# Two pairs of projection blocks by seven products in tiles 3 to 6, and query copies on VectorE behind four strided transposing transfers, in a sparse-attention and bilinear-FFN kernel

## The chip, the cores and the metric

The kernel runs on one core of one Trainium2 chip. A core has TensorE (PE, matrix products into PSUM), VectorE (DVE), ScalarE (ACT) and GpSimd (POOL), and queues from which transfers are issued (here those of SyncE, SP, and of POOL). The metric is device time in microseconds (us), the median of several executions. The kernel before took 326.81 us (three runs: 325.43 to 327.33). One further execution was profiled.

## The reference

```python
# q, k, v: (8, 8, 576, 64); w_a, w_b: (512, 1536); w_out: (1536, 512)
scores = q @ k.T / 8
rel = pos[:, None] - pos[None, :]
mask_local   = (rel >= 0) & (rel < 32)                               # heads 0 to 3
mask_strided = (rel >= 0) & (pos[None, :] % 32 == pos[:, None] % 32) # heads 4 to 7
attn = softmax(where(mask, scores, -1e9))
x = (attn @ v), heads side by side, as (4608, 512)
out = ((x @ w_a) * (x @ w_b)) @ w_out
```

Products are taken in bf16 and summed in fp32.

## The kernel before

**Staging.** The 4608 tokens are nine FFN tiles of 512 (`NT`, t = 0 to 8). Attention runs by batch element b (576 tokens each). The transposed attention output goes into a ring `xT` of four batch elements, [128, 4, 2304], so tile 4 wraps round and its products are cut into 256 columns. The attention of batch b is spread, in small steps, over the FFN of tile b-1.

**The order is written by hand.** Inside the schedule block the program order is the order on each engine. A tile is 16 slots: 12 slots of `ffn_ab` (one 128-wide block f of d_ff each: eight products of 512 columns into two banks, a ScalarE copy `a_sb` of the one, L633, a VectorE product with the other into `pf`, L636) and 4 slots of the second projection (the "y" slots). After each slot, `take(i)` (L1057) emits the attention steps due there (`STEPS` for batches 1 and 2, `LATER` and `IN_Y` for the others, L570 to L578), and `at` holds loads and sums due at that slot (L1001 to L1044). From slot 14 on, POOL first copies one element of the slot's result into `pace` (L1054), so what POOL issues next waits for that slot.

**Attention steps.** S(u): scores into the two-bank tile `st` (L377), exp on ScalarE (L397), mask on VectorE (L415). V(u), u < 4: P times V into `o` (L454), reciprocal and scaling on VectorE (L462, L480). V(u), u >= 4 from batch 2 on is `step_VT`: the product transposed, into two banks `o` (L513), Ln and Exp of the sums on ScalarE (L523, L524), a VectorE product into `xT` (L527). O and I send the local heads' rows out to DRAM and back transposed (L495, L500). Q0 to Q3 are `step_Q`: from batch 2 on, queries arrive transposed by DMA (`step_D`, L320 and L323) in `qT` and POOL copies them into `qz`, whose other 64 partitions are zero: Q0 and Q1 the local heads (L335), Q2 and Q3 the strided heads in two pieces with a permutation of tokens (L333).

**Seven products.** The second projection in tiles 1 to 8 (`FAST_Y`) and the first projection's `w_a` half for some pairs of blocks in tiles 7 and 8 (`FAST_A`, `a_pair`, L667) use a 2 by 2 scheme with seven half-size products in place of eight. It needs sums of weights (`wsum_make`, L648, in tile 6), sums of x (`xsum_make`, L659), and, per pair, five ScalarE copies of 128x256 (L705 to L724), and adds (L713, L722 on VectorE, L717 on POOL). `fast_s` (L740) makes the sums of `pf` (`ps`) for the second projection.

**PSUM.** Eight banks: `st` two, `mm` three, `tp` one, `o` two. Projection banks come from `mm_bank` in turn: three `mm`, then `tp`.

Of the kernel before, what the change touches and what calls it, by code (L numbers as in the profile page):

```python
# [7 lines left out]
F32 = mybir.dt.float32  # L8
# [6 lines left out]
FIRST_D = 2  # L15
# [11 lines left out]
FAST_Y = (1, 2, 3, 4, 5, 6, 7, 8)  # L27
FAST_A = {7: (1, 2, 3, 4, 5), 8: (0, 1, 2, 3, 4, 5)}
# [3 lines left out]
def kernel(  # L32
# [44 lines left out]
    qz_pair = [(const.tile([128, 2, 2, S], BF16, name=f"qz{i}l"), const.tile([128, 2, RS, 2, NP], BF16, name=f"qz{i}s"))  # L77
               for i in range(2)]
    qz_buf = [[(l[:, :, j], s[:, :, :, j]) for j in range(2)] for l, s in qz_pair]
# [30 lines left out]
    def fill_v(t):  # L110
        nc.gpsimd.memset(t[:, :, :, D:] if len(t.shape) == 4 else t[:, :, D:], 1.0)
# [67 lines left out]

    def blocks(nm, z):  # L180
        z = int(z)
        return sb.tile([128, 2, (S, RS * GP)[z]], BF16, tag=f"t{nm}{z}", name=f"t{nm}{z}", bufs=1)
# [133 lines left out]
    def step_D(b, z, nm):  # L316

        rows = nats[b, nm, z == 1]
        if z == 0:
            nc.sync.dma_start(out=kT_buf[b % 2][0][:, :, PAD:] if nm == "k" else qT[0],  # L320
                              in_=rows.rearrange("t h d -> t (h d)"), transpose=True)
        else:
            nc.sync.dma_start(out=kT_strided(b)[:, :HL * W] if nm == "k" else qT[1],  # L323
                              in_=rows.rearrange("h (t e) d -> (h t) (e d)", e=2), transpose=True)

    def step_Q(b, z, j):

        r = slice(64 * j, 64 * j + 64)
        src = qT[z][r]
        if z:  # L330
            src = src.rearrange("d (c h p i) -> d c h i p", c=2, h=2, i=4)
            for c in range(2):
                nc.gpsimd.tensor_copy(qz_buf[b % 2][j][1][r, c].rearrange("d (h i) p -> d h i p", h=2), src[:, c])  # L333
        else:
            nc.gpsimd.tensor_copy(qz_buf[b % 2][j][0][r], src)  # L335
# [22 lines left out]
    def S_p(b, u):  # L358
        c, half, M, n, G = unit(u)
        kT = kT_buf[b % 2][c // 2]  # L360

        st = pst.tile([128, 2, 512], F32, tag="st", name="st")
        held[b, "st", u] = st
        if b > 0:
            sv = st.rearrange("p a (i n) -> p (a i) n", n=256)
            for i in range(G):
                k0 = (G * half + i) * (LW if c < 2 else GP)
                if c < 2:
                    rhs = qz_pair[b % 2][0][:, c % 2, :, k0:k0 + n]
                else:  # L370
                    rhs = qz_pair[b % 2][1][:, c % 2, G * half + i]
                if c < 2 or b < FIRST_D:
                    lhs = kT[:, c % 2, k0:k0 + 128]
                else:
                    k0 = W * (u - HL) + i
                    lhs = kT_strided(b)[:, k0:k0 + 509:4]
                nc.tensor.matmul(sv[:, i, :2 * n].rearrange("p (j n) -> p j n", j=2), lhsT=lhs, rhs=rhs, start=True, stop=True)  # L377
# [49 lines left out]
    def V_p(b, u):  # L427
        c, half, M, n, G = unit(u)
        p = ps.pop((b, u))
        if b == 0:  # L430

            o = psum4["o"].tile([128, 512], F32, tag="o", name="o")
            if c < 2:
                of = o[:, :2 * G * (D + 1)].rearrange("p (j g e) -> p j g e", j=2, e=D + 1)
                sm = of[:, :, :, D:]
            else:
                of = o.rearrange("p (j g e) -> p j g e", j=2, e=D)
                sm = psum4["sum"].tile([128, 2, 4, 1], F32, tag="sum", name="sum")
        else:
            o = psum4["o"].tile([128, 2, 512], F32, tag="o", name="o")  # L440
            of = o[:, :, :G * (D + 1)].rearrange("p j (g e) -> p j g e", e=D + 1)
            sm = of[:, :, :, D:]
# [59 lines left out]
    def step_VT(b, u):  # L502

        c, half, M, n, G = unit(u)
        p = ps.pop((b, u))
        o = psum4["o"].tile([128, 2, 512], F32, tag="o", name="o")
        for i in range(G):
            for j in range(2):
                if c < 2:
                    vt = vl_buf[b % 2][:, (2 * c + j) * 6 + 3 * half + i]  # L510
                else:
                    vt = vs_buf[b % 2][:, u - HL, 2 * i + j]
                nc.tensor.matmul(o[:, j, i * n:(i + 1) * n], lhsT=vt, rhs=p_cols(b, p, j, i, n, n)[:M], start=True, stop=True)  # L513

        r = sb.tile([128, RS * 4 * D], BF16, tag="xr", name="xr", bufs=2)[:64, :4 * W].bitcast(F32)
        r = r.rearrange("p (j w) -> p j w", j=2)
        if c < 2:
            sums = o[64:, :, :W]
        else:

            sums = o[64:, :, :W].rearrange("d j (i p) -> d p i j", p=NP)
            r = r.rearrange("d j w -> d (j w)").rearrange("d (p i j) -> d p i j", i=G, j=2)
        nc.scalar.activation(r, sums, ACT.Ln)  # L523
        nc.scalar.activation(r, r, ACT.Exp, scale=-1.0)  # L524
        if c >= 2:
            dst = xT[64 * (u % 2):64 * (u % 2) + 64, c, S * (b % XR):S * (b % XR + 1)]
            nc.vector.tensor_mul(dst.rearrange("d (p i j) -> d p i j", i=G, j=2),  # L527
                                 o[:64, :, :W].rearrange("d j (i p) -> d p i j", p=NP), r)
            return
        for j in range(2):  # L530
            dst = xT[64 * j:64 * j + 64, c, S * (b % XR):S * (b % XR + 1)]
            nc.vector.tensor_mul(dst[:, W * half:W * (half + 1)], o[:64, j, :W], r[:, j])
# [21 lines left out]
    def step_X(b, c):  # L554
# [20 lines left out]
    LATER = {-6: "Q0", -5: "Q1", -1: "S0", 0: "S1", 1: "V0 Q2", 2: "S2", 3: "V1 O0 Q3", 4: "S3 I0", 5: "V2", 6: "S4", 7: "V3 O1", 8: "S5", 9: "V4 I1",  # L575
# [39 lines left out]
    def ffn_ab(t, f, mid, ab=None):  # L615
# [3 lines left out]
        if f // 2 in FAST_A.get(t, ()):  # L619
            if f % 2 == 0:  # L620
                pairs[t, f // 2] = a_pair(t, f // 2)
            return next(pairs[t, f // 2])
# [9 lines left out]
        a_sb = fsb.tile([128, TTOK], F32, tag="a_sb", name="a_sb")  # L632
# [4 lines left out]
        else:  # L637
# [4 lines left out]
    wsum_a = [flat.rearrange("p (c g m) -> p c g m", c=2, g=FG)  # L642
              for flat in [vl_buf[0].rearrange("p a b -> p (a b)")[:, 12 * 128 * z:12 * 128 * (z + 1)] for z in range(2)]
              + [t[:, :12 * 128] for t in qz_flat[0]]]
    xsum = {t: qz_flat[1][t - 7][:, :8 * HT].rearrange("p (n c m) -> p n c m", n=4, c=2)
            for t in FAST_A}

    def wsum_make(n):  # L648
        w, s_ = (lambda e, j: wav[:, j, :, :, e]), wsum_a
        a, b, op = ((w(1, 0), w(1, 1), ALU.add), (s_[0], w(0, 0), ALU.subtract), (w(0, 0), w(1, 0), ALU.subtract),  # L650
                    (w(0, 1), s_[1], ALU.subtract))[n]
        for c in range(2):
            nc.vector.tensor_tensor(s_[n][:, c], a[:, c], b[:, c], op=op)

    def x_part(t, j, k):
        x0 = TTOK * t % (XR * S) + HT * k
        return xT[:, 2 * j:2 * j + 2, x0:x0 + HT]
# [8 lines left out]

    def a_pair(t, g):  # L667
# [3 lines left out]
        X = pool.tile([128, 2, 512], F32, tag=nm, name="ax")[:, 0, :HT]  # L671
        a = ([fsb.tile([128, TTOK], F32, tag="a_sb", name="a_sb") for _ in range(2)] if g % 2 == 0 else
# [155 lines left out]
    def y_tail(t):  # L828

        plan, y = products(t), y_bufs()  # L830
        banks = {("X", 1): psum4["o"].tile([128, 2, 512], F32, tag="o", name="end")[:, 0, :HN],
# [75 lines left out]
    with tc.manual_schedule(engines={ENG.PE, ENG.SP, ENG.Pool, ENG.DVE, ENG.Activation}):  # L907
# [72 lines left out]
        open_psum(ctx, mm=3, tp=1, o=1)  # L980
# [41 lines left out]
        for n in range(4):  # L1022
            do(16 * (NT - 3) + 2 * n + 2, wsum_make, n)
# [11 lines left out]
        do(28, fill_v, vs_buf[1])  # L1035
# [52 lines left out]
```

## Time and profile before

| what | value |
|---|---|
| median of three runs | 326.81 us |
| the profiled execution's own time | 326.64 us |
| its span, first to last instruction | 324.9 us |
| mean granted TensorE clock | 0.997 |
| PE busy | 315.5 us (97%) |
| VectorE busy | 234.1 us (72%) |
| ScalarE busy | 186.4 us (57%) |
| POOL busy | 150.1 us (46%) |
| chain that ended last: PE / VectorE / ScalarE | 89% / 4% / 2% |

A matmul's record includes its pipeline, so PE at 97% is not PE at its peak; durations of chains of matmuls are better read from the starts of successive pieces in the chain that ended last. Tile boundaries in that chain are at about 57.9 us (tile 1), 94.5 (tile 2), 128.4 (3), 161.8 (4), 195.9 (5), 229.6 (6) and 263.0 (7).

### The profile page before, as it was taken

Reading aid. Unit: us, or ns where it says so; the run is one execution under the profiler, and the core shown is the slowest. Engines: PE = TensorE matmul, PEld = TensorE weight load, DVE = VectorE, ACT = ScalarE, POOL = GpSimd, SP = SyncE. Lnnn points to the kernel's source line nnn. Section 1 sums busy time; section 2 is a strip of 40 time slices with the busy share of each in tenths; the row PEclk is TensorE's granted clock in tenths of the full one; section 3 lists DMA queues with packets and bytes.
Section 4 is the critical chain, followed back from the end, with each engine's and each line's share of the span. In section 5 each row is a group of like instructions: output and inputs, shape, how many; then the busy total and the mean of one; then the engine's idle time right before and its main releaser. Section 6 shows DMA issues by size and latency. Waiting matters only on the chain.

```text
span 324.9 us, 7111 instructions
## 1 busy us (share of the span) xinstructions
PE 315.5 (97%) x2706; PEld 214.2 (66%) x2734; DVE 234.1 (72%) x489; ACT 186.4 (57%) x331; POOL 150.1 (46%) x240
## 2 busy tenths in 40 slices
PE   8999999998999999999999999999999999999994
PEld 6754555454765578556999995559555866786684
DVE  6765786498956785688667766777699667857862
ACT  6763766454754476447644765467546655535541
POOL 8944922893785356524652565336124003202520
PEclk9999999999999999999999999999999999999998
DMA  8999999999699999999998999999863030004004
GB/s 150 155 204 196 204 187 204 204 126 175 87 132 153 191 129 101 131 207 167 102 104 181 158 107 107 158 182 112 59 101 103 2 113 17 3 2 129 0 3 129
DMA packets 127234, 40.40 MB, mean 124 GB/s; under 512 B 115040, under 2 KB 124320, under 8 KB 127008
## 3 DMA queue, kind: packets, MB, share of 16 engines
q0 software_dynamic: 80400, 19.28, 64.5%
q1 hardware_dynamic: 46656, 20.61, 36.3%
q8 instruction: 21, 0.34, 0.5%
q14 instruction: 13, 0.11, 0.1%
q10 hardware_dynamic: 144, 0.07, 0.1%
HBM read 39.12 MB, written 18.28 MB: 177 GB/s over the span
## 4 chain that ended last, share of the span: by engine, by line
PE 89%; DVE 4%; ACT 2%; issue 2%; DMA 2%; POOL 0%; ACTq 0%; POOLq 0%
PE mm L612 42%; PE mm L816 18%; PE mm L696 5%; PE st L377 4%; PE mm L878 3%; PE ax L689 3%; PE o L454 2%; PE mm L689 2%; PE o L513 2%; DMA shared<-in_q_dram 2%; PE mm L843 2%; PE end L843 1%; DVE p L415 1%; PE misc L156 1%; PE tp L540 1%
## 5 line engine op out<-in xcount | busy, mean ns | idle before, releaser
L612 PE MATMUL mm<-xT,wb_sb 128*128 128x512 bf16 (+1 forms) x381 | 88.0, 352 | 0.4
L612 PE MATMUL mm<-xT,wa_sb 128*128 128x512 bf16 (+1 forms) x367 | 86.6, 351 | 0.6
L633 ACT COPY a_sb<-mm 128x512 f32<-128x512 f32 x84 | 49.2, 585 | 47.1 <-PE mm L612 45.5
L636 DVE TENSOR_TENSOR pf<-a_sb,mm 128x512 bf16<-128x512 f32 x74 | 50.6, 684 | 26.0 <-PE mm L612 18.4
L612 PEld LDWEIGHTS <-wb_sb 128*128 128x128 bf16 x392 | 37.8, 98 | 33.7 <-issue 0.4
L1054 POOL CAST pace<-pf 1x1 f32<-1x1 bf16 x72 | 21.0, 291 | 77.0 <-DVE pf L636 47.8
L612 PEld LDWEIGHTS <-wa_sb 128*128 128x128 bf16 x392 | 34.9, 98 | 20.9
L397 ACT ACTIVATE p<-st 72x576 bf16<-72x576 f32 (+1 forms) x56 | 36.4, 650 | 20.1 <-PE st L377 19.8
L816 PEld LDWEIGHTS <-ps 128*128 128x128 bf16 x336 | 32.5, 98 | 4.6 <-issue 0.5
L527 DVE TENSOR_TENSOR xT<-o,xr 64x576 bf16<-64x576 f32 x24 | 18.0, 751 | 19.8 <-ACT xr L524 19.6
L816 PE MATMUL mm<-wf,ps 128*128 128x256 bf16 x252 | 30.1, 273 | 0.5 <-ACT y_sb L781 0.3
L781 ACT COPY y_sb<-mm 128x512 f32<-128x512 f32 (+1 forms) x32 | 17.9, 559 | 19.3 <-PE mm L816 16.6
L816 PEld LDWEIGHTS <-pf 128*128 128x128 bf16 x252 | 23.6, 98 | 2.7
L696 PE MATMUL mm<-xT,wb_sb 128*128 128x512 bf16 x83 | 25.3, 379 | 0.1
L816 PE MATMUL mm<-wo_sb,pf 128*128 128x256 bf16 x168 | 21.8, 273 | 0.0
L750 DVE TENSOR_TENSOR ps<-pf 128x512 bf16<-128x512 bf16 (+1 forms) x49 | 21.2, 433 | 0.7
L523 ACT ACTIVATE xr<-o 64x576 f32<-64x576 f32 x24 | 15.6, 648 | 9.4 <-PE o L513 9.2
L1054 POOL COPY pace<-y_sb 1x1 f32<-1x1 f32 x17 | 4.1, 241 | 36.0 <-ACT y_sb L887 13.3
L236 POOL DMA_DIRECT2D vs<-in_v_dram x24 | 20.4, 863 | 0.0
L415 DVE TENSOR_TENSOR p<-p,mask_s 72x576 int16<-72x576 int16 x28 | 18.7, 669 | 1.8 <-ACT p L397 1.5
L454 PEld LDWEIGHTS <-p 128*128 128x128 bf16 (+1 forms) x256 | 13.0, 97 | 8.9 <-DVE xl L480 2.1
L415 DVE TENSOR_TENSOR p<-p,mask_l 128x576 int16<-128x576 int16 x32 | 14.7, 458 | 4.3 <-ACT p L397 4.3
(183 smaller groups left out, 546.7 us busy)
## 6 DMA issues: line engine op xcount, KB each, us to landing
out_dram<-y_sb SPq DMA_DIRECT2D x14, 512.0 KB, 4.9
kr<-in_k_dram POOLq DMA_DIRECT2D x12, 288.0 KB, 5.8
qr<-in_q_dram POOLq DMA_DIRECT2D x12, 288.0 KB, 6.9
vl<-in_v_dram POOLq DMA_DIRECT2D x6, 384.0 KB, 9.5
out_dram<-y_sb SPq DMA_DIRECT2D x7, 256.0 KB, 4.1
vs<-in_v_dram POOLq DMA_DIRECT2D x24, 72.0 KB, 5.9
xd<-xl SPq DMA_DIRECT2D x12, 144.0 KB, 4.8
wo_sb<-in_moe_w_out_dram POOLq DMA_DIRECT2D x4, 384.0 KB, 10.4
```

Of the source, the lines that this page charges most:

```text
L236: nc.gpsimd.dma_start(out=vs_buf[b % 2][:, h, :, 0:D], in_=v[b, HL + h].rearrange("(p r) d -> p r d", r=RS))
L397: nc.scalar.activation(p_flat(p)[:M, :2 * W].rearrange("p (i n) -> p i n", n=2 * n), st[:M].rearrange("p a (i n) -> p (a i) n", n=256)[:, ...
L415: nc.vector.tensor_tensor(pi, pi, mk, op=ALU.bitwise_and)
L454: nc.tensor.matmul(of[:, j, i, :w], lhsT=pt, rhs=vt, start=True, stop=True)
L527: nc.vector.tensor_mul(dst.rearrange("d (p i j) -> d p i j", i=G, j=2), o[:64, :, :W].rearrange("d j (i p) -> d p i j", p=NP), r)
L612: nc.tensor.matmul(ps_[:, c0:c0 + n], lhsT=w[:, kk, 128 * f:128 * (f + 1)], rhs=xT[:, kk, x0:x0 + n], start=(kk == first and c0 == 0), sto ...
L633: nc.scalar.copy(a_sb, ab[0])
L636: nc.vector.tensor_mul(pf[:, f, :].rearrange("p (i a s) -> p a i s", i=2, s=16), halves(a_sb), halves(ab[1]))
L696: nc.tensor.matmul(got[e], lhsT=wb_sb[:, kk, 128 * f:128 * (f + 1)], rhs=xT[:, kk, x0:x0 + TTOK], start=kk == 0, stop=kk == KD - 1)
L750: nc.vector.tensor_tensor(s[:, n], a, b, op=op)
L816: nc.tensor.matmul(bank[b][:, q], lhsT=lhs(g, q), rhs=rhs(g), start=k in "172" and q == 0 and g == 0, stop=g == FG - 1, skip_group_check=True)
L1054: nc.gpsimd.tensor_copy(pace, done)
```

## The change

- `MID_A`: in tiles 3 to 6, block pairs g = 1 and 3 (f = 2, 3 and 6, 7) go through a new `a_pair_mid`, seven products for the `w_a` half. Its accumulating chain X is a 256-column tile in a bank of its own, tag `e`; all adds are on VectorE. Sums of x for these tiles are made in slot 16t-1 and 16t; sums of weights are made in tile 2 (slots 34 to 47) in place of tile 6, in buffers that attention used early.
- From slot 48 (tile 3) on, `o` is one bank, and `e` the other. `V_p` fits one bank then; `step_VT` writes its two halves to `o` and `e`, with two Ln and two products of half size. In all `step_VT` the loops of i and j change places.
- `step_Q` is one VectorE copy of 64x1152 for each of Q0 to Q3; the token permutation of the strided heads is now made by four transposing transfers of 288 rows each in place of one of 1152. `qz`'s strided part has another layout, and the scores read it accordingly.
- Q steps move: Q0, Q1 two slots later (into the y slots; batch 2: from 16.5 to 17), Q2, Q3 one slot later (batch 2: from 20 and 21 to 21.5 and 22). Three loads move by one slot; the memset of `vs`'s spare columns for the odd buffer moves from slot 28 to slot 2. `a_sb` has three buffers.

```diff
+MID_A = {t: (1, 3) for t in (3, 4, 5, 6)}
...
-    qz_pair = [(... name=f"qz{i}l"), const.tile([128, 2, RS, 2, NP], BF16, name=f"qz{i}s"))
+    qz_pair = [(... name=f"qz{i}l"), const.tile([128, 2, 2, RS, NP], BF16, name=f"qz{i}s"))
...
         else:
-            nc.sync.dma_start(out=kT_strided(b)[:, :HL * W] if nm == "k" else qT[1],
-                              in_=rows.rearrange("h (t e) d -> (h t) (e d)", e=2), transpose=True)
+            for i in range(4):
+                nc.sync.dma_start(out=qT[1][:, W * i:W * (i + 1)], transpose=True,
+                                  in_=rows.rearrange("h (p i e) d -> i (h p) (e d)", i=4, e=2)[i])
 
     def step_Q(b, z, j):
         r = slice(64 * j, 64 * j + 64)
-        src = qT[z][r]
-        if z:
-            src = src.rearrange("d (c h p i) -> d c h i p", c=2, h=2, i=4)
-            for c in range(2):
-                nc.gpsimd.tensor_copy(qz_buf[b % 2][j][1][r, c].rearrange("d (h i) p -> d h i p", h=2), src[:, c])
-        else:
-            nc.gpsimd.tensor_copy(qz_buf[b % 2][j][0][r], src)
+        dst = qz_buf[b % 2][j][z][r]
+        nc.vector.tensor_copy(dst.rearrange("d c r n -> d (c r n)") if z else dst, qT[z][r])
...
+        if "e" in psum4:
+            o = [psum4[nm].tile([128, 512], F32, tag=nm, name=nm) for nm in "oe"]
...
+        for j in range(2):
+            for i in range(G):
+                nc.tensor.matmul(o[j][:, i * n:(i + 1) * n], lhsT=vs_buf[b % 2][:, u - HL, 2 * i + j],
+                                 rhs=p_cols(b, p, j, i, n, n)[:M], start=True, stop=True)
...
+        for j in range(2):
+            nc.scalar.activation(by_token(r)[:, :, :, j], o[j][64:, :W].rearrange("d (i p) -> d p i", p=NP), ACT.Ln)
+        nc.scalar.activation(r, r, ACT.Exp, scale=-1.0)
+        for j in range(2):
+            nc.vector.tensor_mul(by_token(dst)[:, :, :, j], o[j][:64, :W].rearrange("d (i p) -> d p i", p=NP),
+                                 by_token(r)[:, :, :, j])
...
-             2: {16.5: "Q0 Q1", 20: "S0 Q2", 20.5: "S1", 21: "V0 Q3", 21.5: "S2", 22: "V1", 22.5: "S3 O0", ...
+             2: {17: "Q0 Q1", 20: "S0", 20.5: "S1", 21: "V0", 21.5: "S2 Q2", 22: "V1 Q3", 22.5: "S3 O0", ...
-    LATER = {-6: "Q0", -5: "Q1", -1: "S0", 0: "S1", 1: "V0 Q2", 2: "S2", 3: "V1 O0 Q3", 4: "S3 I0", ...
+    LATER = {-4: "Q0", -3: "Q1", -1: "S0", 0: "S1", 1: "V0", 2: "S2 Q2", 3: "V1 O0", 4: "S3 I0 Q3", ...
...
+    def a_pair_mid(t, g):
+        pf = pfs[t]
+        X = psum4["e"].tile([128, 512], F32, tag="e", name="e")[:, :HT]
+        Y, Z, b1, b0 = [mm_bank([128, TTOK]) for _ in range(4)]
...
+        P(Y, w(0, 1), x(1, 0), True)
+        P(X, w(0, 0), x(0, 0), True)
+        nc.scalar.copy(quarter(0, 0), X)
+        b_mm(b1, 1, (0, 1, 2))
+        P(X, ws(1), xs(1))
+        nc.scalar.copy(quarter(1, 0), X)
+        P(Z, ws(2), xs(2), True)
+        nc.scalar.copy(p7, Z)
+        b_mm(b1, 1, (3,))
+        add(quarter(0, 0), Y)
+        yield p7[:1, :1]
+        P(X, ws(0), xs(0))
+        nc.scalar.copy(quarter(1, 1), X)
+        b_mm(b0, 0, (0,))
+        P(Z, w(1, 1), xs(3))
+        add(quarter(1, 0), Z)
+        add(quarter(1, 1), p7)
+        b_mm(b0, 0, (1, 2, 3))
+        P(X, ws(3), x(1, 1))
+        nc.scalar.copy(quarter(0, 1), X)
+        mult(1, b1)
+        mult(0, b0)
+        yield pf[:1, 2 * g, :1]
...
-                do(15, load_vl, b)
+                do(14, load_vl, b)
-                do(17 if b == FIRST_D + 1 else g0 - 2, load_qk, b, False)
+                do(18 if b == FIRST_D + 1 else g0 - 2, load_qk, b, False)
...
         for n in range(4):
-            do(16 * (NT - 3) + 2 * n + 2, wsum_make, n)
+            for c in range(2):
+                do(16 * 2 + (2, 5, 7, 9, 11, 13, 14, 15)[2 * n + c], wsum_make, n, c)
+        for t in MID_A:
+            do(16 * t - 1, xsum_make, t, 0)
+            for n in (1, 2, 3):
+                do(16 * t, xsum_make, t, n)
...
-        do(28, fill_v, vs_buf[1])
+        do(2, fill_v, vs_buf[1])
...
+            elif i == 16 * min(MID_A):
+                outs.close()
+                open_psum(ctx, o=1, e=1)
```

Here P(bank, ...) is two products of 256 columns, `b_mm` one of 512 columns for each entry, `add` a VectorE sum of 128x256 fp32, `mult` the VectorE product into `pf`.

More of the change, by code (lines that the diff above doesn't have):

```diff
@@ L110, in fill_v @@
     def fill_v(t):
-        nc.gpsimd.memset(t[:, :, :, D:] if len(t.shape) == 4 else t[:, :, D:], 1.0)
+        nc.gpsimd.memset(t[:, :, :, D + 1:], 1.0)
     spare = const.tile([128, 2], BF16, name="spare")
@@ L505, in step_VT @@
         p = ps.pop((b, u))
[L506 to L513, printed above, removed]
-        r = sb.tile([128, RS * 4 * D], BF16, tag="xr", name="xr", bufs=2)[:64, :4 * W].bitcast(F32)
@@ L516, in step_VT @@
[L516 to L528, printed above, removed]
+        if "e" in psum4:
+            o = [psum4[nm].tile([128, 512], F32, tag=nm, name=nm) for nm in "oe"]
+        else:
+            o2 = psum4["o"].tile([128, 2, 512], F32, tag="o", name="o")
+            o = [o2[:, j] for j in range(2)]
@@ L631, in ffn_ab @@
                 ab_mm(t, f, ab, range(KD), mid)
-        a_sb = fsb.tile([128, TTOK], F32, tag="a_sb", name="a_sb")
+        a_sb = fsb.tile([128, TTOK], F32, tag="a_sb", name="a_sb", bufs=3)
         nc.scalar.copy(a_sb, ab[0])
@@ L670, in a_pair @@
         pool, nm = ((pst, "st"), (psum4["o"], "o"))[g % 2]
-        X = pool.tile([128, 2, 512], F32, tag=nm, name="ax")[:, 0, :HT]
-        a = ([fsb.tile([128, TTOK], F32, tag="a_sb", name="a_sb") for _ in range(2)] if g % 2 == 0 else
+        X = pool.tile([128, 512] if nm == "o" else [128, 2, 512], F32, tag=nm, name="ax")
+        X = X[:, :HT] if nm == "o" else X[:, 0, :HT]
+        a = ([fsb.tile([128, TTOK], F32, tag="a_sb", name="a_sb", bufs=3) for _ in range(2)] if g % 2 == 0 else
              [t.rearrange("p h n -> p (h n)")[:, :2 * TTOK].bitcast(F32) for t in kT_buf[0]])
@@ L830, in y_tail @@
         plan, y = products(t), y_bufs()
-        banks = {("X", 1): psum4["o"].tile([128, 2, 512], F32, tag="o", name="end")[:, 0, :HN],
+        banks = {("X", 1): psum4["o"].tile([128, 512], F32, tag="o", name="end")[:, :HN],
                  ("Z", 1): pst.tile([128, 2, 512], F32, tag="st", name="end")[:, 0, :HN]}
@@ L979 @@
         early.close()
-        open_psum(ctx, mm=3, tp=1, o=1)
+        open_psum(ctx, mm=3, tp=1)
+        outs = ExitStack()
+        open_psum(outs, o=1)
         slots = []
```

83 lines of the change are left out of this document (63 added, 20 removed), and 2 rows, old and new, of the table STEPS.

## The prediction

> **What bounds the kernel now.** I read the page's chain of waits first.
>
> ```profile
> PE 89%; DVE 4%; ACT 2%; issue 2%; DMA 2%; POOL 0%; ACTq 0%; POOLq 0%
> ```
>
> TensorE's own work sets the end, with two exceptions: the prologue, which the change leaves alone, and tile 1. So an edit can gain in two ways: fewer TensorE columns anywhere, or fewer TensorE waits in tile 1. The table of stages separates them (columns: stretch, its length, busy us and instructions of PE, PEld, DVE, ACT, POOL, granted clock, DMA share, GB/s):
>
> ```profile
> 68.00:74.50 6.50, 5.37 (x44) 2.89 (x44) 6.43 (x12) 3.34 (x6) 6.44 (x13) 1.00 1.90 126
> 82.90:94.50 11.60, 10.95 (x115) 9.32 (x112) 9.05 (x14) 7.27 (x13) 10.68 (x14) 1.00 1.31 119
> 94.50:117.90 23.40, 23.24 (x156) 12.17 (x158) 16.80 (x35) 13.05 (x22) 10.15 (x20) 1.00 1.38 154
> 117.90:128.40 10.50, 10.45 (x110) 9.32 (x108) 7.77 (x13) 7.37 (x12) 7.42 (x11) 1.00 1.37 100
> ```
>
> Rows 2 and 4 are the y slots of tiles 1 and 2, with the same TensorE work; tile 1 takes 11.6 us for them, tile 2 10.5. In row 1 TensorE idles 1.1 us while VectorE and POOL are both full. The timeline says why (start, us, engine, line, instruction; the bracket is idle time and its releaser):
>
> ```profile
> 70.42 2.04 DVE L750 TENSOR_TENSOR ps<-pf 128x512 bf16<-128x512 bf16 x1
> 70.67 1.50 POOL L333 COPY qz0s<-qTs 64x576 bf16<-64x576 bf16 x2
> 74.18 0.35 PE L454 MATMUL o<-vl,p 128*128 128x65 bf16 x6 [1.07 <-DVE xl L480]
> ...
> 83.17 1.52 DVE L415 TENSOR_TENSOR p<-p,mask_s 72x576 int16<-72x576 int16 x1
> 83.24 1.14 POOL L335 COPY qz1l<-qTl 64x1152 bf16<-64x1152 bf16 x1
> ...
> 100.00 1.35 POOL L333 COPY qz1s<-qTs 64x576 bf16<-64x576 bf16 x2 [3.35 <-DMA qTs<-qr]
> ```
>
> L750's median is 0.42 us and L415's with mask_s 0.45; beside a POOL query copy they take 2.04 and 1.52, as long as the copy runs and their own work after it. VectorE is then late and PE waits 1.07 us for it. The last row: POOL also waits for the transposed queries to land; today nobody waits for POOL there.
>
> **Part 1, the seven products.** A plain block is eight 512-column products, 1.73 us in the chain (row 137.88 below), so a pair is 3.46. Tile 7's seven-product pairs are the same mix of products; one piece of each pair recurs here:
>
> ```profile
> 137.88 1.73 PE mm L612 x8
> ...
> 266.48 0.65 PE mm L696 x3
> 269.74 0.65 PE mm L696 x3
> 272.99 0.65 PE mm L696 x3
> ```
>
> The distance is 3.26 us, so 0.20 less for each pair and 1.2 for six pairs; in tile 4, where all columns come in 256s (16 for 1.75 us, 0.109 each), 32 become 30, 0.22 less, for two pairs. Together 1.65 us off the path, if no copy is late. What is added beside it, for each pair: five ScalarE copies of 0.373 (L705 to L724) for two of 0.585, +0.70 us; VectorE adds 3 x 0.425 (L713, L722, L779 at 256 columns), +1.28. For each tile four sums of x, 4 x 0.42 (L663), +1.68. The weight sums, 8 x 0.55 (L653), move from tile 6 to tile 2. `step_VT` for batches 4 to 7: two Ln of 64x288 for one of 0.648: between 128x256 and 128x512 copies (0.373 and 0.585) the slope gives about 0.40 each, +0.15; two products for one of 0.751, about 0.43 each by the 256-column adds, +0.11. The third `a_sb` buffer, the bank split and the new loop order add no instruction on TensorE: zero, and there is nothing to uncover.
>
> The tightest place is the chain in the one-bank tile. In slot 3, X must be copied out before the last X product. ScalarE first does the exp of S2: it starts 0.44 us after the first score product (67.52 to 67.96), takes 0.65, then the copy 0.37, 1.5 us with a little signalling. TensorE in that time does the scores 0.30, two 256s 0.22, one 512 0.22, two 256s 0.22, three 512s 0.65, in all 1.6. Cover 0.1 us; the same in slot 7. Bounds: 0 (tile 7 shows none) to 0.65 for each of 8 (a whole exp in the way). I take 0.1 in all, since the cover is short but there. If the copy is late, the next is only the rest of this pair.
>
> **Part 2, the query copies.** POOL loses 32.5 us (L333 9.5 + 8.4, L335 7.3 + 7.3). VectorE gains 24 copies. No VectorE row has this shape; the nearest are L269's, 96x768 in bf16: 0.345 three times and 1.04 once. The once is beside POOL issuing transfers:
>
> ```profile
> 40.44 1.04 DVE L269 COPY tq<-shared 96x768 bf16<-96x768 bf16 x1
> ...
> 39.17 2.13 POOL L207 DMA_DIRECT2D qr<-in_q_dram  x1
> 40.27 1.55 POOL L205 DMA_DIRECT2D kr<-in_k_dram  x1
> ```
>
> So 0.35 to 1.14 (POOL's own time for 64x1152); I take 0.345 x 1152/768 = 0.52, since most rows are undisturbed. That is 2.1 us of VectorE for each batch, against about 1.0 to 1.6 of stretched masks and sums that go.
>
> The Trainium skill, "SBUF — State Buffer", section "Who interferes with whom", has this as an exclusive lock: a VectorE instruction with two SBUF inputs and a GpSimd one that reads SBUF shut each other out. Here the trace agrees (0.45 to 1.52). It goes on that VectorE's fast copies shut out descriptor generation too, whoever starts first, which speaks against the change; the 1.04 us row agrees. By it every Q copy that meets a load being issued would take about 1.0.
>
> In tile 1 VectorE is the limit twice. Around 70 to 74 it loses 1.62 (2.04 to 0.42) and 0.38 (L750 at 74.04 took 0.79) and gains two copies, 1.04: 0.96 less, so of the 1.07 us wait I take 0.95. In the y slots it loses 1.07 and 0.54 (L415 at 83.17 and 87.35) and gains Q0, Q1 of batch 3, 1.04: 0.57 less, so of the 1.1 us I take 0.6. Together 1.55; bounds 0 (the new copies fill the hole) and 2.2.
>
> From tile 2 on VectorE has 23.4 - 16.8 = 6.6 us free in slots 0 to 11. In tiles 3 to 6 it gets there 3 x 0.42 + 2 x 1.28 + 2 x 0.52 + 0.2 = 5.1; in tile 2, 5 x 0.55 + 1.04 = 3.8. That is cover, and the cost is nothing. Gone, it is `pf` and `ps` that come late, and the y products wait.
>
> **Part 3, the four transfers.** SP issues three more for each of six batches. Its rows: 1.30 to 1.67 us for 1152 rows, 1.15 for 576 (L500), so up to 3 x 1.15 = 3.5 us more of SP each time. Behind them on SP stands only the next tile's first store (from 92.8 to 103.6 in tile 1-2, later 128.1 to 137.2), so SP has room. But the copy Q2 needs all four, and now VectorE waits, with masks, `pf` and reciprocals queued behind. How much later the last lands is not shown. Below: nothing, as the bytes are the same. Above: 8.4 us, if each takes the 2.8 us that lay between the landings of kT0s and qTs (59.66 + 5.7 and 61.07 + 7.1). I take 1.5, by the 1.15 us issue of the nearest small one with landings overlapped. Slack of the old landing to the place where VectorE comes to Q2: batch 2, 68.2 to 71.3, 3.1; batch 3, 99.95 to about 101.5, less what tile 1 gains, about 1 (SP's chain moves up with it in part); batches 4, 6 and 7, about 3 (131.4, 199.2, 233.0 against slot ends of tile 3, 5, 6); batch 5 more. A VectorE halt of some 2 us costs nothing: the product of slot 3 (0.69) is needed by the second half of slot 5. So only batch 3 may pay: 0.2.
>
> **The moved loads and memset.** They sit on POOL, 46% busy before and less after; they land well ahead of use (kr of batch 3 is issued at 66.3, transposed at 71.6, read at 94.2). Zero; without that cover the transposes of the batch would slip one slot, about 2 us, against the same slack.
>
> **Sum.** 326.64 - 1.65 + 0.1 - 1.55 + 0.2 = 323.7; the profiled execution stands 0.17 under the median of 326.81, so I forecast 323.8.
>
> **Rivals.**
> - *Tile 1 loses all its waits:* 2.2 in place of 1.55, the chain tight but never late: 323.0 and, with the loads earlier on a freer POOL, down to 322.4. For: POOL is full there (6.44 of 6.50). Against: VectorE was full too and takes over the copies.
> - *Only one of the two gains arrives.* Either ScalarE's copies come late by 0.2 in each pair (the cover is 0.1), or VectorE's new copies are held by POOL's issuing (two more of 1.04) and fill tile 1's hole. Each gives 325.3 to 325.5. That the lockout merely changes its partner is how the change would not do what it says.
> - *VectorE stands before the query copies (slower).* If the last of four transfers lands 5.5 us later (nearly 2 us for each extra one), VectorE halts for 2.4 in batch 2, about 4.5 or more in batch 3 and 2.5 in 4, 6 and 7; less the 2.0 that banks allow, PE loses 0.4 + 2.5 to 3.5 + 3 x 0.5, about 5.4: 329.2. It decides from about 3 us later on in batch 3 and 5 us in the others. For: 10.8 us to land in batch 3, and POOL waited 13.1 us in four places for qTs. Against: the bytes are unchanged, and issues overlap landings in every pair of rows above.
>
> **Chances.** Forecast 0.48 (own range 322.8 to 325.0), tile 1 free 0.12, one gain only 0.24, slower 0.16. A measurement can tell 0.5%, 1.6 us: below 325.2 is faster, above 328.4 slower. Faster: 0.46 + 0.12 + 0.05 = 0.63. Same: 0.02 + 0.19 = 0.21. Slower: 0.16. The range leaves out the slower case and the tip of the fast one: 322.0 to 327.5.
>
> **What would show it.** Right: no mask or `ps` sum beyond 0.7 us after 58 us; tile 1 about 1.5 us shorter; tiles 3, 5, 6 about 0.4 shorter each; query copies near 0.5. Wrong: VectorE idle before a copy with qTs as releaser and PE waiting for `pf` or `xl` behind it; PE waiting for an `a_sb` copy out of `e`; copies of 1 us beside POOL's issues.

## The result, and the profile after

The changed kernel took 325.53 us, the median of 21 executions (323.89 to 339.45), beside 327.06 us for the kernel before (21 executions, 325.43 to 331.09): a ratio of 0.9943, with a 95% interval of 0.9926 to 0.9959. That is 1.9 us gained by the ratio, where 3.0 us were forecast. The execution that was profiled with this result was a disturbed one (339.45 us), so the lines below come from a second profile of the same kernel, of an execution of 323.95 us with a span of 322.2 us. In the job of that profile the changed kernel stood at 0.993 (0.9906 to 0.9954).

First the chain of waits of the changed kernel:

```profile
PE 84%; DMA 7%; DVE 3%; ACT 2%; SPq 2%; issue 1%; DVEq 0%
```

Before, the chain held 2% of DMA; now it holds 7%. TensorE is busy 98% of the span, so most of these DMA pieces lie under work of TensorE that was issued anyway, but two of them matter below (the rows of `xT`, and `qTs`).

The same four stretches as in the prediction, moved to the new starts of the slots (columns as there):

```profile
68.00:74.50 6.50, 6.50 (x53) 3.55 (x52) 6.37 (x16) 3.29 (x7) 4.91 (x10) 1.00 1.72 111
81.90:92.60 10.70, 10.38 (x113) 9.27 (x110) 8.31 (x16) 7.05 (x13) 7.24 (x10) 1.00 1.56 121
92.60:116.50 23.90, 23.54 (x158) 12.06 (x156) 18.21 (x40) 13.21 (x22) 7.17 (x15) 1.00 1.18 161
116.50:126.80 10.30, 10.30 (x115) 9.36 (x112) 8.80 (x18) 6.99 (x12) 4.74 (x9) 1.00 1.84 123
```

Row 1: TensorE now works all of the 6.50 us, 5.37 before, with VectorE as full as it was. Row 2: the y slots of tile 1 take 10.7 us from their first product to the first of tile 2, where they took 11.4 (82.95 to 94.30; the stretch of 11.6 in the prediction was cut a little wider). Row 3 is longer than before (23.9 for 23.4): here something was given back.

The timeline of the changed kernel (start, us, engine, line, instruction, and in the bracket idle time and its releaser) shows both sides:

```profile
70.26 0.41 DVE L820 TENSOR_TENSOR ps<-pf 128x512 bf16<-128x512 bf16 x1
71.02 0.52 DVE L338 COPY qz0s<-qTs 64x1152 bf16<-64x1152 bf16 x1
...
93.95 0.38 PE L617 MATMUL mm<-xT,wa_sb 128*128 128x512 bf16 x1 [0.36 <-DMA xT<-xd]
...
101.62 0.45 DVE L338 COPY qz1s<-qTs 64x1152 bf16<-64x1152 bf16 x1 [1.34 <-DMA qTs<-qr]
...
133.37 0.37 ACT L724 COPY a_sb<-e 128x256 f32<-128x256 f32 x1
```

The `ps` sum that took 2.04 us beside a POOL copy takes 0.41, and the query copy that joined VectorE takes 0.52. New is the third line: the first projection of tile 2 waits for the transposed rows of batch 2. It had not waited before. The fourth line is VectorE waiting for the four strided transfers, which was expected; no wait of TensorE follows it here.

The starts of the stages, read from the first products of each, give a balance (us; tile 1 and so on are lengths, and the last row ends with TensorE's last product). The last two columns are experiments told below; "best" is the last of them:

| stage | before | changed | without the pairs | best |
|---|---|---|---|---|
| start of tile 1 | 57.7 | 57.3 | 57.9 | 57.8 |
| tile 1 | 36.6 | 35.3 | 34.9 | 34.9 |
| tile 2 | 33.7 | 34.2 | 33.8 | 33.7 |
| tiles 3 to 6 | 134.7 | 133.3 | 134.7 | 133.0 |
| from tile 7 on | 58.0 | 58.0 | 58.2 | 58.0 |

In the profiled execution tile 1 gained 1.3 and tiles 3 to 6 gained 1.4; tile 2 lost 0.5. The 0.4 gained ahead of tile 1 has no cause in the change that these rows show: that start moves by as much between the other kernels.

### The profile page after: what moved, and what is told of

Its sections match the earlier page's. It is cut to its first block, busy times and chain, and to the rows that moved or that the text cites. A ratio compares the mean times of both kernels' runs of the same rounds, so it can differ in the third digit from the quotient of the medians.

```text
span 337.7 us, 7313 instructions
## 1 busy us (share of the span) xinstructions
PE 320.3 (95%) x2766; PEld 219.4 (65%) x2766; DVE 251.7 (75%) x569; ACT 191.9 (57%) x371; POOL 120.5 (36%) x210
## 2 busy tenths in 40 slices
DMA packets 127811, 40.41 MB, mean 120 GB/s; under 512 B 115616, under 2 KB 124896, under 8 KB 127584
## 4 chain that ended last, share of the span: by engine, by line
PE 81%; DMA 8%; DVE 4%; POOL 2%; issue 1%; ACT 1%; SPq 1%; DVEq 0%; POOLq 0%
PE mm L617 32%; PE mm L886 16%; PE mm L766 5%; PE st L381 4%; PE mm L702 4%; PE mm L948 3%; PE ax L759 3%; PE o L462 2%; PE mm L759 2%; DMA shared<-in_q_dram 2%; DMA xd<-xl 2%; DMA qTs<-qr 2%; PE e L688 2%; DMA xT<-xd 2%; PE mm L913 2%; PE mm L688 1%
## 5 line engine op out<-in xcount | busy, mean ns | idle before, releaser
L617 PE MATMUL mm<-xT,wa_sb 128*128 128x512 bf16 (+1 forms) x304 | 73.8, 363 | 4.7 <-DMA xT<-xd 4.7
L617 PE MATMUL mm<-xT,wb_sb 128*128 128x512 bf16 (+1 forms) x304 | 73.3, 361 | 1.6 <-DVE a_sb L710 1.6
L638 ACT COPY a_sb<-mm 128x512 f32<-128x512 f32 x68 | 39.8, 585 | 35.7 <-PE mm L617 33.9
L1134 POOL CAST pace<-pf 1x1 f32<-1x1 bf16 x67 | 18.5, 277 | 100.8 <-DVE pf L641 52.6
L617 PEld LDWEIGHTS <-wb_sb 128*128 128x128 bf16 x312 | 30.4, 99 | 35.1 <-issue 8.8
L641 DVE TENSOR_TENSOR pf<-a_sb,mm 128x512 bf16<-128x512 f32 x58 | 39.3, 679 | 14.4 <-ACT a_sb L638 10.7
L401 ACT ACTIVATE p<-st 72x576 bf16<-72x576 f32 (+1 forms) x56 | 36.4, 650 | 22.2 <-PE st L381 21.5
L617 PEld LDWEIGHTS <-wa_sb 128*128 128x128 bf16 x312 | 28.2, 99 | 18.4 <-issue 1.0
L1134 POOL COPY pace<-y_sb 1x1 f32<-1x1 f32 x21 | 9.2, 436 | 55.5 <-DVE y_sb L849 22.3
L462 PEld LDWEIGHTS <-p 128*128 128x128 bf16 (+1 forms) x256 | 13.4, 99 | 10.7 <-DVE xr L488 3.1
L820 DVE TENSOR_TENSOR ps<-pf 128x512 bf16<-128x512 bf16 (+1 forms) x49 | 19.6, 399 | 0.8
L702 PE MATMUL mm<-xT,wb_sb 128*128 128x512 bf16 (+1 forms) x80 | 19.1, 336 | 0.0
L536 DVE TENSOR_TENSOR xT<-o,xr 64x288 bf16<-64x288 f32 x16 | 7.7, 479 | 13.5 <-ACT xr L534 13.4
L419 DVE TENSOR_TENSOR p<-p,mask_s 72x576 int16<-72x576 int16 x28 | 12.6, 450 | 1.9 <-ACT p L401 1.7
```

Of the source, the lines that this page charges most:

```text
L401: nc.scalar.activation(p_flat(p)[:M, :2 * W].rearrange("p (i n) -> p i n", n=2 * n), st[:M].rearrange("p a (i n) -> p (a i) n", n=256)[:, ...
L419: nc.vector.tensor_tensor(pi, pi, mk, op=ALU.bitwise_and)
L462: nc.tensor.matmul(of[:, j, i, :w], lhsT=pt, rhs=vt, start=True, stop=True)
L617: nc.tensor.matmul(ps_[:, c0:c0 + n], lhsT=w[:, kk, 128 * f:128 * (f + 1)], rhs=xT[:, kk, x0:x0 + n], start=(kk == first and c0 == 0), sto ...
L638: nc.scalar.copy(a_sb, ab[0])
L641: nc.vector.tensor_mul(pf[:, f, :].rearrange("p (i a s) -> p a i s", i=2, s=16), halves(a_sb), halves(ab[1]))
```

## The experiments

Twelve kernels ran, in four jobs; the kernel before ran in each job, with medians of 326.6 to 326.8 us, and every ratio is against it. The changed kernel was run again in the first of them alone, with the next three experiments, so kernels of the other jobs are set beside it by their ratios. All twelve compute the whole reference.

### The changed kernel again

No edit; its profile is the one shown above.

> The changed kernel itself, for a profile whose transfers land in their usual time. Against the kernel before: 1.5 us less, 0.994, by the times so far. My theory: the pairs give 1.65 us in all (tiles 3, 5 and 6 each 0.4 shorter), so tile 1 gives nothing net, because its waits are still there or reappear as another wait in tile 0 or 1. Rival: tile 1 is about 1.5 us shorter as forecast, and something in tiles 2 to 6 takes 1.4 us back, which would be seen as waits of PE for VectorE there.

324.48 us, ratio 0.993 (0.9906 to 0.9954). The balance above speaks for the rival: tile 1 is shorter by 1.3 us. Of what something else was to take back 0.5 us is seen, in tile 2, and there TensorE waits for a transfer and not for VectorE.

### Without the seven-product pairs

```diff
-MID_A = {t: (1, 3) for t in (3, 4, 5, 6)}
+MID_A = {}
...
-            elif i == 16 * min(MID_A):
+            elif i == 48:
```

> The changed kernel with no pair of tiles 3 to 6 by seven products (no sums of x for them); the one-bank split, the query copies on VectorE and the four transfers stay. If the pairs give 1.65 us and the rest nothing: 0.999 to 1.000 of the kernel before. If the query part gives the 1.55 us that was forecast: 0.995, and the pairs then give no more than 0.3 us.

0.9981 (0.996 to 1.0003). The same job has the changed kernel at 0.993, so the pairs are worth a factor of 0.9949, about 1.7 us, where 1.65 was forecast; the two intervals leave about 1 us of doubt either way. The stages are sharper: tiles 3 to 6 last 134.7 us without the pairs, as before the change, and 133.3 with them in the changed kernel. The bank split, the halves of `step_VT` and the VectorE query copies alone add nothing there. What is left, 0.9981, is 0.6 us for the query part (from nothing to 1.3 by its interval), where 1.55 less 0.2 was forecast. This is where the forecast lost in the ratios. In the profiled execution the gain is there: tile 1 is 1.7 us shorter, and only 0.15 of it is given back in tile 2.

### The query part alone, and the pairs alone

The first is the kernel before with the edits of `step_D`, `step_Q`, `qz`, the steps and the moved loads and memset. The second is the changed kernel with these undone, save for the loads and the memset:

```diff
-        dst = qz_buf[b % 2][j][z][r]
-        nc.vector.tensor_copy(dst.rearrange("d c r n -> d (c r n)") if z else dst, qT[z][r])
+        src = qT[z][r]
...
+                nc.gpsimd.tensor_copy(qz_buf[b % 2][j][1][r, c].rearrange("d (h i) p -> d h i p", h=2), src[:, c])
...
-    LATER = {-4: "Q0", -3: "Q1", -1: "S0", 0: "S1", 1: "V0", 2: "S2 Q2", 3: "V1 O0", 4: "S3 I0 Q3", ...
+    LATER = {-6: "Q0", -5: "Q1", -1: "S0", 0: "S1", 1: "V0 Q2", 2: "S2", 3: "V1 O0 Q3", 4: "S3 I0", ...
```

> The kernel before with the query part alone (copies on VectorE, four transfers, moved steps, moved loads and memset), without pairs and without the bank split. Forecast of record: tile 1 shorter by 1.55 us, 0.995. Rival, that the hole in VectorE's time is filled again by the new copies or by another lockout: 1.000, with PE waits of about 1 us in tile 1 or tile 0.

> The changed kernel with the query part undone (POOL copies the queries, one transfer, the steps where they were); pairs, bank split and moved loads stay. If the two parts are independent and the pairs give 1.65 us: 0.995. If the pairs need the query part, because POOL copies stretch the sums and masks by 1 us in tiles with little VectorE time left: 0.997 to 1.000, with stretched masks beside POOL copies in tiles 3 to 6 and PE waits behind them.

The query part alone: 0.9987 (0.996 to 1.0014), no gain that can be told from none; its profiled execution, 329.53 us, has a tile 1 of 34.9 us, 1.7 shorter than before, but began tile 1 3.4 us late and shows TensorE waiting 1.1 us for `xT`. The pairs alone: 0.9972 (0.9951 to 0.9992), less than their 1.7 us; in that profile TensorE waits 1.37 us for a POOL copy of `qz0l` and 0.7 us for `xT`, tile 2 lasts 34.5 us, and tiles 3 to 6 take 133.9, half of the pairs' gain. What takes the other half without the query part isn't settled: the next kernel has POOL copies too, in the new steps and layout, and takes 133.0 there. So the parts do not simply add up (0.9987 times 0.9972 is 0.9959, the whole is 0.993, though the intervals overlap), and both carry the wait for `xT`, which is not in the profile of the kernel before.

### The engine of the query copies

```diff
-        nc.vector.tensor_copy(dst.rearrange("d c r n -> d (c r n)") if z else dst, qT[z][r])
+        nc.gpsimd.tensor_copy(dst.rearrange("d c r n -> d (c r n)") if z else dst, qT[z][r])
```

> The changed kernel with the contiguous query copies put on POOL again; four transfers, steps, pairs and loads stay. If the lockout between POOL copies and VectorE is what tile 1 gained from: masks and sums of 1 to 2 us beside POOL copies, tile 1 longer by 1.3 us or more, 0.997 to 0.998. Rival, that the four transfers and the moved steps bring tile 1's gain: 0.993.

0.9978 (0.9954 to 1.0003), and tile 1 is back at 36.4 us. The timeline of this kernel:

```profile
73.06 1.78 DVE L820 TENSOR_TENSOR ps<-ps,pf 128x512 bf16<-128x512 bf16 x1
73.11 1.44 POOL L338 COPY qz0s<-qTs 64x1152 bf16<-64x1152 bf16 x1
...
75.89 0.41 PE L381 MATMUL st<-qz0s,kT0s 128*128 128x144 bf16 x4 [1.25 <-POOL qz0s L338]
```

The stretched sum returns beside the POOL copy, and TensorE now waits for the copy itself. That the gain of tile 1 comes from the engine of these copies, and not from the other edits, is shown by this one line of difference.

### Query copies one step later

Q2 and Q3 of every batch from 2 on one slot later, for instance:

```diff
-    LATER = {-4: "Q0", -3: "Q1", -1: "S0", 0: "S1", 1: "V0", 2: "S2 Q2", 3: "V1 O0", 4: "S3 I0 Q3", 5: "V2", ...
+    LATER = {-4: "Q0", -3: "Q1", -1: "S0", 0: "S1", 1: "V0", 2: "S2", 3: "V1 O0 Q2", 4: "S3 I0", 5: "V2 Q3", ...
```

> The changed kernel with Q2 and Q3 one step later (batch 2: 22 and 22.5; others: slots 3 and 5). VectorE waited 2.0 us for qTs in two places of the changed kernel's profile. If these waits reach PE (my 0.2 us for batch 3, or more): 0.2 to 0.5 us less, 0.991 to 0.992, and no VectorE wait for qTs. If the banks cover them: 0.993, as the changed kernel.

0.9996 (0.9971 to 1.002): the whole gain gone. VectorE waits for `qTs` no more, but five times TensorE waits about 0.2 us before scores for a query copy that now comes just ahead of them, 1.0 us in sum, and it waits 1.43 us for `xT` in tile 2. So a later copy moves the waits for `qTs` to TensorE.

### The loads of v, earlier and later

The change leaves the loads of `vs` and `vl` for batch 3 in their slots, but a POOL without query copies comes to them sooner: the first two are issued at 82.70 and 83.56 us, 84.33 and 85.20 before. This kernel issues them still earlier, the next one later:

```diff
-                    do(g0 + h + 10, load_vs, b, (h,))
-                do(g0 + (10 if b == FIRST_D + 1 else 7), load_vl, b)
+                    do((23, 23, 24, 24)[h] if b == FIRST_D + 1 else g0 + h + 10, load_vs, b, (h,))
+                do(g0 + (6 if b == FIRST_D + 1 else 7), load_vl, b)
```

> The changed kernel with batch 3's v loads issued earlier (vl at slot 22 in place of 26, the four vs at 23, 23, 24, 24 in place of 26 to 29). My theory: freed of its copies, POOL issues vs and vl at 82.7 to 85 us, before and beside batch 2's row store xd (84.2), where they stood behind a copy before; the store then lands in 3.9 us in place of 2.2 and the transpose in 5.8, and the first products of tile 2 wait for xT (0.36 us in the profile). With the loads gone from there: no wait of PE for xT, 0.4 us less in the profile, and 0.991 to 0.993 of the kernel before (changed kernel: 0.993). Rival: the store lands late for another reason (the transposes ahead of it on SP); then nothing moves, or tile 1 loses by loads beside the earlier store.

The gain expected of it missed: 1.0127 (1.0081 to 1.0173), slower than the kernel before. The timeline of this kernel, SyncE's queue and then TensorE, says how:

```profile
80.14 0.94 SPq L503 DMA_DIRECT2D xd<-xl  x1
89.39 1.16 SPq L508 DMA_TRANSPOSE xT<-xd  x1
90.64 1.00 SPq L503 DMA_DIRECT2D xd<-xl  x1
...
101.33 0.58 PE L617 MATMUL mm<-xT,wa_sb 128*128 128x512 bf16 x1 [5.75 <-DMA xT<-xd]
```

The two stores of rows (`xd`) and the two transposes that bring them back (`xT`) go through SyncE in order. POOL issued the five loads of v from 74.89 to 80.80. Beside them the first store, issued at 80.14, is read back only at 89.39, and the second store can't be issued before 90.64. TensorE pays 5.75 us. It is the wait of 0.36 us above, made large.

```diff
-                    do(g0 + h + 10, load_vs, b, (h,))
-                do(g0 + (10 if b == FIRST_D + 1 else 7), load_vl, b)
+                    do(g0 + h + (13 if b == FIRST_D + 1 else 10), load_vs, b, (h,))
+                do(g0 + (12 if b == FIRST_D + 1 else 7), load_vl, b)
```

> The changed kernel with batch 3's v loads later (vl at slot 28, vs at 29 to 32, in place of 26 and 26 to 29). Issued 8 us earlier, they made PE wait 5.8 us for xT; the same mechanism the other way says: stores and transposes land in 2 to 4 us, no wait for xT, 0.990 to 0.992. But kT1s and qTs of batch 3 then share the engines with the loads: if qTs lands more than 2 us after VectorE comes to Q2, PE waits for pf behind it, up to 1.8 us, 0.995.

0.9964 (0.9936 to 0.9991), no better than the changed kernel's 0.993, so the expectation missed. Its profiled execution, 323.04 us, has no wait for `xT`. SyncE's queue there has the two transposes at 72.21 and 76.34, which take 7.3 us to issue, and then the second store and its read-back:

```profile
83.30 0.53 SPq L503 DMA_DIRECT2D xd<-xl  x1
85.46 1.14 SPq L508 DMA_TRANSPOSE xT<-xd  x1
```

With no load of v ahead of it the store is read back after 2.2 us, 3.9 in the changed kernel. What the other executions waited for isn't seen, so for the time this experiment is inconclusive.

### The old places of the loads and the memset

```diff
-                do(14, load_vl, b)
+                do(15, load_vl, b)
-                do(18 if b == FIRST_D + 1 else g0 - 2, load_qk, b, False)
+                do(17 if b == FIRST_D + 1 else g0 - 2, load_qk, b, False)
-        do(2, fill_v, vs_buf[1])
+        do(28, fill_v, vs_buf[1])
```

(The memset covers one more column again, as before.)

> The changed kernel with the three loads and the memset of the spare columns where they were (vl of batch 2 at slot 15, kr and qr of batch 3 at 17, memset at 28). I costed these moves at nothing: 0.993, as the changed kernel. Rival: the vl load at slot 14 goes ahead of qTl's transposing transfer (7.9 us to land, VectorE waited 1.7 us for it at slot 17); with it back, Q0 comes without a wait and tile 1 is up to 0.5 us shorter: 0.991. Other rival: kr and qr at 17 meet the copies' old place: 0.995.

0.9936 (0.9904 to 0.9967), the changed kernel's own ratio. Six of its twelve executions lie between 322.98 and 323.91 us; the profiled one, 326.75 us, shows two waits that such an execution can't have paid in full (timeline):

```profile
105.20 0.45 DVE L338 COPY qz1s<-qTs 64x1152 bf16<-64x1152 bf16 x1 [3.84 <-DMA qTs<-qr]
106.77 1.02 PE L617 MATMUL mm<-xT,wb_sb 128*128 128x512 bf16 x4 [1.84 <-DVE pf L641]
```

VectorE stood 3.84 us before the query copy and TensorE 1.84 us behind it, a tolerance of 2.0 us. It also waited 1.61 us for `xT`. The order of the transfers around 80 to 90 us is thus not fixed by the places of the loads alone.

### The rows ahead of the keys and queries

In SyncE's queue of the changed kernel the transposes of `kT1l` and `qTl` for batch 3 stand ahead of the first store of batch 2's rows. One slot later for both puts the store first:

```diff
-            gs = {2: (13, 14, 15, 15), 3: (6, 6, 14, 15)}.get(b) or (3, 4, 10, 11)
+            gs = {2: (13, 14, 15, 15), 3: (7, 7, 14, 15)}.get(b) or (3, 4, 10, 11)
```

> The changed kernel with batch 3's transposing transfers kT1l and qTl one slot later (slot 23 in place of 22), so that on SP batch 2's first row store (rows ready at 72.8 us, issued at 80.6 behind them) goes ahead of them. My theory now: the end of tile 1 hangs on SP's chain store, transpose, store, transpose; what stands ahead of it (transposes whose issue takes 3.5 us in a full queue, v loads) decides when tile 2 gets its xT. Then the second store is issued at about 82 in place of 84.2, no wait of PE for xT, 0.990 to 0.992 of the kernel before. Rival: the wait is the landing time in shared DMA engines whatever the order; then 0.993 to 0.994, and xT lands no earlier.

0.9912 (0.9887 to 0.9937), 323.45 us, and no wait for `xT`. SyncE's queue in the changed kernel, and then what POOL issues there (timeline):

```profile
72.41 4.39 SPq L325 DMA_TRANSPOSE kT1l<-kr  x1
76.91 3.60 SPq L325 DMA_TRANSPOSE qTl<-qr  x1
80.60 0.53 SPq L503 DMA_DIRECT2D xd<-xl  x1
...
84.20 0.53 SPq L503 DMA_DIRECT2D xd<-xl  x1
88.10 1.14 SPq L508 DMA_TRANSPOSE xT<-xd  x1
```

```profile
82.70 0.87 POOL L241 DMA_DIRECT2D vs<-in_v_dram  x1 [0.48 <-issue]
83.56 1.47 POOL L223 DMA_DIRECT2D vl<-in_v_dram  x1
```

and SyncE's in this experiment:

```profile
73.47 0.34 SPq L503 DMA_DIRECT2D xd<-xl  x1
...
82.31 0.53 SPq L503 DMA_DIRECT2D xd<-xl  x1
84.60 1.14 SPq L508 DMA_TRANSPOSE xT<-xd  x1
```

The kernel before, SyncE's and then POOL's:

```profile
84.04 0.57 SPq L495 DMA_DIRECT2D xd<-xl  x1
86.27 1.15 SPq L500 DMA_TRANSPOSE xT<-xd  x1
...
84.33 0.88 POOL L236 DMA_DIRECT2D vs<-in_v_dram  x1
85.20 1.47 POOL L218 DMA_DIRECT2D vl<-in_v_dram  x1
```

The rows of the first store are ready at 72.8, but in the changed kernel SyncE spends 8.0 us issuing two transposes and stores them at 80.60. Compared with the kernel before, nothing is lost by that yet: its first store, issued at 75.50, was read back at 82.83, this one at 82.95, and the second store goes out at 84.20 for 84.04. The delay comes behind it. In the changed kernel two loads of v are issued ahead of the second store, and it is read back 3.9 us later; in the kernel before they stood behind the store, which was read back after 2.2. With the rows first the second store goes out at 82.31, ahead of the loads (83.32), and is read back after 2.3 us.

The profiles of all these kernels agree. In six of them loads of v had been on their way for 0.3 us or more when the second store was issued, and it was read back after 3.6 to 6.0 us; in the other seven, the kernel before among them, after 2.2 to 2.9.

```diff
-                 24: "V3 I0 O1", 24.5: "S5", ...
+                 24: "V3 O1 I0", 24.5: "S5", ...
```

> The changed kernel with kT1l and qTl one slot later and, for batch 2, the second row store ahead of the first transpose on SP (O1 before I0), so that no store waits for another's landing. By the theory of SP's chain: second store at about 81, xT landed before 90, no wait of PE for xT, 0.989 to 0.991. Rival: as for the run before, 0.993 to 0.994.

The second store ahead of the first read-back as well: 0.9922 (0.99 to 0.9944), 323.65 us, above the expected 0.989 to 0.991 and nothing on top of the edit before. Its profiled execution, 326.45 us, lost 2.7 us in tile 0 (TensorE waiting twice for `tq`), and shows what the memset that the change moved to slot 2 can do (timeline):

```profile
42.33 2.86 DVE L245 COPY vs<-tk 72x512 bf16<-72x512 bf16 x1
...
42.70 2.34 POOL L112 MEMSET vs<- 72x2016 bf16 x1
```

### Both together

The rows first, and the old places of the loads and the memset.

> The run with the row store ahead of kT1l and qTl, and the three loads and the memset where they were before the change. Theory: the memset at slot 2 runs at 42.2 to 44.0 us in tile 0 and holds VectorE's copies (2.42 us for 0.35 and 2.86 for 0.28 in two profiles; PE waited 1.6 and 2.7 us there); the transposes ahead of the store are the other wait. With both gone: no copy above 1.1 us in tile 0, no PE wait for xT, 0.989 to 0.991 of the kernel before. Rival: the loads at their old slots bring the waits for xT and qTs back that their run showed (1.6 and 1.8 us): 0.993 to 0.994.

0.9919 (0.989 to 0.9947), 323.41 us, a little above what was expected, ten of twelve executions between 322.84 and 323.76. No wait for `xT`, and in the balance above tile 1 is 1.7 us shorter than before and tiles 3 to 6 are 1.6 shorter: the forecast's two terms (1.55 and 1.65), with nothing given back. It is faster than the kernel before, and its median is the lowest of the kernels told of here, but its interval overlaps those of the changed kernel and of the rows alone, so that the memset's old place adds something is not shown. The three kernels with the rows first stand at 0.9912 to 0.9922 and the changed kernel at 0.9943 and 0.993: a gain in time is likely, but their intervals overlap. That the wait for `xT` is gone is seen in the profile of each of the three.

## Why the prediction was right, and what it missed

**The direction and the range** held: faster by 0.57%, 325.53 in 322.0 to 327.5. The forecast itself, 323.8, was 1.7 us too low in time, and 325.53 lies outside its own narrower range of 322.8 to 325.0. (The terms as written give 323.9.) The profiled execution of the changed kernel, 323.95 us, is at the forecast. Of the 21 executions six lie at 323.89 to 324.39 and eight at 325.49 to 325.77; what those eight paid isn't profiled, so most of the 1.7 us has no shown cause.

**Part 1, seven products: right in size.** 1.65 us were forecast, and the kernel without the pairs puts them at 1.7. Tiles 3, 5 and 6 became 0.40 us shorter each, as forecast; tile 4 gained 0.16 in the changed kernel and 0.44 in the best one. The chain of waits of the changed kernel in tile 3 has the block ahead of the pair and the one behind it:

```profile
128.89 1.73 PE mm L617 x8
...
134.49 1.73 PE mm L617 x8
```

That is 5.60 us; the rows of the kernel before (130.11 and, three blocks on, 135.90) were 5.79 apart, so 0.19 less for the pair, 0.20 forecast. The tight place, the copy of X in slot 3, ended at 133.74 (133.37 and 0.37 in the timeline above) for a product that starts at 133.92 in the same timeline: 0.2 us of cover, 0.1 forecast. The two copies ahead of it leave less, 0.07 and 0.11, and there is no wait for `e` in any of the profiles. The halves of `step_VT` were priced at 0.40 and 0.43; they measured 0.41 to 0.43 (Ln) and 0.46 to 0.48 (product).

**Part 2, the query copies: right in mechanism and size.** The copies take 0.45 to 0.54 on average in the changed kernel, 0.52 forecast. L820's sums are at 0.42 on average (L750's were 0.456), the strided masks at 0.45 (0.669 before). Tile 1 gained 1.3 to 1.7 us in the profiles, for 1.55, and 0.2 when POOL makes the copies (36.4 for 36.6). In the best kernel it gained 1.0 ahead of the y slots and 0.7 in them, for 0.95 and 0.6. The price feared for these copies did come where the memset kept its old place: two copies of that kernel took 2.11 and 1.63 us beside POOL's work, and TensorE did not wait for them.

**Part 3, the four transfers: right for batch 3, the slack too large later.** SyncE issues the four in 6.09 us in the changed kernel and in 5.07 with the rows first (up to 3.5 more than the 1.5 of one was forecast). The reading of SyncE's rows as 1.30 to 1.67 us left out longer ones of the kernel before: 3.67 for `qTs` at 89.14, and up to 3.13 for a `kT0l`. In tile 2 VectorE waits 1.34 us for them and TensorE nothing, and the experiment with a wait of 3.84 us put the tolerance at the 2.0 that was assumed. In tiles 3 to 6 the tolerance is smaller, since Q2 now stands in VectorE's order ahead of the pair's sum L710, which frees a bank for the next slot: in tile 4 VectorE waits 0.68 us, the copy of `qz1s` runs at 167.96, the sum behind it until 168.75, and TensorE goes on at 168.80. Tile 4 took 33.8 us there and 33.5 in the best kernel. "Batches 4, 6 and 7, about 3" of slack was not all there was to say.

**What the sum left out: the path of the rows through SyncE's queue.** "The moved loads and memset ... Zero" is not the step that failed: with all four undone the ratio is the changed kernel's own. The text had no term for what a POOL without query copies issues sooner, save as a gain ("with the loads earlier on a freer POOL, down to 322.4"), and of the queue it said that "SP has room" and that "SP's chain moves up with it in part". But tile 2 needs batch 2's rows, which go through that queue as two stores and two transposes back, and the chain did not move up. Before, the last of the rows landed at 92.85 us for products at 95.17, 2.3 us of cover. In the changed kernel tile 2 begins 1.7 us sooner (92.56 for 94.30), and the rows land 1.1 later, at 93.91, behind the loads of v. The products come at 93.95, 0.5 us late, and that is what tile 2 lost. TensorE's wait is 0.36 us in this profile and 0.7 to 1.6 in four of the others (none in those without the pairs and with POOL's copies); forcing the collision raised it to 5.75, and both the rows first and the later loads took it away in their profiles. In the profiled execution it explains 0.5 us, not the 1.7 of the median. Why the two transposes take longer to issue than the 3.0 us of the kernel before isn't settled: their sum is 5.1 to 8.1 us in all twelve kernels, and no single part of the change is common to all of them.

**The rivals.** "Only one of the two gains arrives" came near in time (325.3 to 325.5), but not by its mechanism as far as the profiles go: both gains are there, and a new wait took some of them back. "VectorE stands before the query copies" happened in single executions, with its price (3.84 less 2.0), but is not the common case. "Tile 1 loses all its waits" did not come true: the best kernel's tile 1 gained 1.7 us, nearer to the 1.55 of the forecast than to 2.2.

## What to carry to other kernels

When an engine is freed of work off the critical path, ask what it will issue earlier, and what those transfers will run beside: here a load landing sooner was no gain, and it delayed a small store on which the next tile depended. Follow each chain that goes out to memory and back through its queue, with everything that stands ahead of it in program order; place the short stores of such a chain before the long transposes. An instruction put into an in-order engine's list ahead of one that frees a buffer has less slack than the arrival of its own data suggests.

## What the runs showed of the hardware

The issue time of a transposing transfer on SyncE is no constant: the same two transfers (`kT1l` and `qTl` of batch 3) took 1.50 and 1.48 us in the kernel before, 4.39 and 3.60 in the changed one, 1.50 and 5.38 with the rows first.

A small store issued on SyncE is not independent of loads issued by POOL: the same store of 144 KB was read back 2.2 us after its issue with the loads of v behind it, and 3.9 us after it with two of them ahead.

A memset on POOL, which only writes, held a VectorE copy for as long as it ran: 2.86 us beside 2.34 (above), and 2.42 beside a memset of 1.80 us in the kernel with the early loads, where the same two copies otherwise take 0.28 and 0.35. The Trainium skill, "SBUF — State Buffer", section "Who interferes with whom", states that VectorE's copies in a two-port mode and GpSimd shut each other out for the whole instruction; these rows agree. The same rule made a case against the query copies, by POOL's issuing: in these profiles the copy at 71.02 ran while POOL issued loads (70.45 for 1.37 us, 71.53 for 0.84) and took 0.52, so of the price of about 1.0 nothing was seen there. In tile 0 of the best kernel a copy did take 1.10, at 40.46 beside an issue of 1.48 at 40.41. When the rule bites and when not, these profiles don't tell.
